# Mixing spread over five steps, sums moved to GpSimd, two products exchanged

## The chip, the cores and the metric

One core of a Trainium2 chip runs the whole program. The metric is the device time of one execution in microseconds; several executions were timed, and one was profiled. The engines go by their short names: PE is TensorE (PEld its weight loads), DVE is VectorE, ACT is ScalarE, POOL is GpSimd, and SP issues most DMAs.

## The reference, cut to what matters

```python
# attention, 8 batches x 8 heads, 576 rows of 64
scores = scale * q @ k.T
scores = where(scores >= max(scores) - tau, scores, -1e9)
x = concat_heads(softmax(scores) @ v)              # (8, 576, 512)
# mixing and channel block
mixed = real(fft(fft(x, axis=1), axis=2))
u = x + mixed
un = (u - mean(u)) / sqrt(var(u) + 1e-6)           # over the 512 channels
out = u + relu(un @ w_ch1) @ w_ch2                 # 512 -> 2048 -> 512
```

## The kernel before, in words

**Attention.** The loop over i runs through 160 steps: 8 batches of 4 head pairs (`NPAIR`) of 5 row tiles (`NT`). In step i, `scores(i)` multiplies one tile of q with the pair's k into two PSUM tiles (`sc`, L434 and L445), and `softmax(i)` takes the row maxima on DVE (`neg`, L462), the exponentials on ACT (`e`, L470), the threshold with the row sum on DVE (L478), and the division (L494). The weights of step i - 1 are transposed on PE (`pe`, `pw`, L540 and L559) and copied out by ACT (`ends`, `e_t`, L547 and L561). When the weights of two tiles stand, `weighted_values(n, 0)` multiplies the first 256 rows with v (`pv`, L582) in the pair's third step (t = 2); `weighted_values(n, 1)` does the other 320 in the first step of the next pair (t = 0). The result goes from PSUM into `x`, a tile of its own for each of the four pairs of a batch (`x0` to `x3`, one buffer each, L588 or L590).

**Folding.** `fold_rows` adds and subtracts a pair's x with its mirror image in a room called `half` (L615; one buffer, also used for `swap`, through which two rows change places by four DMAs in pairs of odd number) and writes `f` (L620 to L629). It runs on POOL, for the last pair of a batch on DVE.

**Mixing.** `mixing(b)` is a generator. It first combines f on DVE (L644 to L672), and yields three times for that. Then come eleven units, a yield behind each: six `py` products over the channels (L683, copied by ACT into `y_e` and `y_o`, L688 and L693) and five `pa`/`pb` products over the sequence (L700, L704). The second sort is followed by ACT's copy into `tmp` (L715; one buffer), two DVE operations (L719, L720) and POOL's additions of x into `u_t` (L722, L726). `u_t` is u transposed, a ring of two batches. Mixing reads all four x tiles of its batch until its last additions are done.

**Channel work.** Groups of 256 rows (16 of them, from g = 2 on) compute both products with seven instead of eight block products; the other blocks' sums make up for the eighth. In `hidden_in_quarters`, `sums` forms the sums of u's quarters (`t_u`, and one block of `u_t` in place, L891), `weights` the sums of the first weights (`s_w`, L900), and `product(m, part)` one of seven products (`ph`, L917) for one half of the hidden units. Products 1, 6 and 7 accumulate in one PSUM bank that is held from 1 to 7; DVE adds what they give to `hs` (L926), ACT copies or applies the relu (L931 and on). Groups alternate between two orders: up starts with product 5, down with product 3. The output stage `channels_in_quarters` does the same for the second product (`po`, L1058), with POOL's `s_form` (L1054), DVE's `combine` (L1019) and DVE's `rows.add` (L795). All matmuls but the scores share four PSUM banks (tag `mm`).

**Order.** From step 40 on, PE executes in the order in which the program is written; a planner orders the other engines' queues, taking what is ready in its own reckoning by order of writing. Up to step 40 all engines keep the written order. Between the parts of a step stand three calls of `fill()`, called stretches here. Each adds `per_slot` to a budget, takes units of mixing and then units of channel work until the budget is spent; channel work of batch b is allowed once its mixing is finished (`mixed`). `start_batch(b)` appends a batch's mixing and groups at the end of the step with i % 20 == 0. Then:

```python
if i < total:
    mix(3)
    pace = iter((0, 2, 2, 2, 2, 4))
```

that is, DVE's part at once, nothing in the next stretch, and then two units in each of four stretches and the rest in the sixth. The last batch (i = 160) has no pace and takes one unit per stretch.

Of the kernel before, what the change touches and what calls it, by code (L numbers as in the profile page):

```python
# [9 lines left out]
FP32 = mybir.dt.float32  # L10
INT32 = mybir.dt.int32
UINT32 = mybir.dt.uint32
ALU = mybir.AluOpType
# [34 lines left out]
def kernel(  # L48
# [12 lines left out]
    nc = tc.nc  # L61
    B, H, S, D = q.shape
# [3 lines left out]
    NPAIR = H // 2  # L66
# [316 lines left out]
    xs = {}  # L383
# [184 lines left out]
    def weighted_values(n, part):  # L568

        b, p = n // NPAIR, PAIRS[n % NPAIR]  # L570
        _, _, vt, e_t, ends, recs = heads[n]
        if part == 0:
            if n % NPAIR == 0:
                xs[b] = [None] * NPAIR
            xs[b][p] = sb.tile([128, S], FP32, tag=f"x{p}", bufs=1, name=f"x{p}")
        x = xs[b][p]
        m = (256, S - 256)[part]
        cols = slice(256 * part, 256 * part + m)
        pv = ps.tile([128, 512], FP32, tag="mm", bufs=4, name="pv")
        for c in range(5):  # L580
            for j in range(2):
                nc.tensor.matmul(  # L582
                    pv[64 * j : 64 * j + 64, 0:m], vt[:, 2 * c + j, :],
                    e_t[:, 4 * j + c, 0:m] if c < 4 else ends[:, 0:m],
                    start=(c == 0), stop=(c == 4), skip_group_check=True,
                )
        if normalized(n):
            nc.scalar.copy(x[:, cols], pv[:, 0:m])  # L588
        else:
            nc.vector.tensor_tensor(  # L590
                out=x[:, cols], in0=pv[:, 0:m], in1=recs[:, 0:m], op=ALU.mult
            )
        if part == 0:
            return
        heads.pop(n)
        if p % 2:

            swap = sb.tile([2, S], FP32, tag="half", bufs=1, name="swap")
            for j in range(2):
                nc.sync.dma_start(out=swap[j : j + 1, :], in_=x[64 * j : 64 * j + 1, :])  # L600
            for j in range(2):
                nc.sync.dma_start(out=x[64 * j : 64 * j + 1, :], in_=swap[1 - j : 2 - j, :])
# [276 lines left out]
    def hidden_in_quarters(g, rows, quarter):  # L879


        c0 = tokens_of(g)[0] % RING
        c1 = (c0 + 128) % RING
        up = (g - FIRST) % 2 == 0
        b = [[[u_t[:, 2 * k + c, z : z + 128] for c in range(2)] for z in (c0, c1)]
             for k in range(2)]
        t1, t2, minus_t4 = ([t_u[:, m, c, :] for c in range(2)] for m in range(3))

        def sums(out_, in0, in1):
            for c in range(2):  # L890
                nc.vector.tensor_tensor(out=out_[c], in0=in0[c], in1=in1[c], op=ALU.subtract)  # L891

        sums(t1, b[0][1], b[0][0])
        sums(t2, b[1][1], t1)
        sums(minus_t4, b[1][0], t2)

        def weights(eng, part, in0, in1, op=ALU.subtract):
            cols = slice(512 * part, 512 * part + 512)
            for c in range(2):
                eng.tensor_tensor(  # L900
                    out=s_u[c][:, cols], in0=in0[c][:, cols], in1=in1[c][:, cols], op=op
                )

        OPERANDS = {
            1: (a_w1[0][0], b[0][0]), 2: (a_w1[0][1], b[1][0]), 3: (s_u, b[1][1]),
            4: (a_w1[1][1], minus_t4), 5: (s_u, t1), 6: (s_u, t2), 7: (a_w1[1][0], b[0][1]),
        }
        banks = {}

        def product(m, part):  # L910
            name = "sum" if m in (1, 6, 7) else m
            if m not in (6, 7):
                banks[name] = ps.tile([128, 512], FP32, tag="mm", bufs=4, name="ph")
            left, right = OPERANDS[m]
            for q in range(4):
                for c in range(2):
                    nc.tensor.matmul(  # L917
                        banks[name][:, 128 * q : 128 * q + 128],
                        left[c][:, 512 * part + 128 * q : 512 * part + 128 * q + 128], right[c],
                        start=q == 0 and c == 0 and m not in (6, 7), stop=c == 1,  # L920
                        skip_group_check=True,
                    )
            return banks[name][:, :]

        def add(to, bank, other=None):
            nc.vector.tensor_tensor(  # L926
                out=to, in0=bank, in1=to if other is None else other, op=ALU.add
            )

        def relu(to):  # L930
            nc.scalar.activation(out=to, in_=to, func=ACT.Relu)  # L931

        def fifth(part):
            y = product(5, part)
            h01, h11 = quarter(1, 0, part), quarter(1, 1, part)
            if up:
                nc.scalar.copy(h11, y)

                weights(nc.gpsimd, part, s_u, a_w1[0][0])
            else:  # L940
                add(h01, y)
                relu(h01)
                add(h11, y)
                relu(h11)

        def third(part):
            y = product(3, part)
            h01 = quarter(1, 0, part)
            if up:
                add(h01, y)  # L950
                relu(h01)
            else:
                nc.scalar.copy(h01, y)
                weights(nc.gpsimd, part, a_w1[1][1], a_w1[1][0])

        def first_two(part):
            h00 = quarter(0, 0, part)
            nc.scalar.copy(h00, product(1, part))
            yield 4096
            add(h00, product(2, part))  # L960
            relu(h00)
            yield 4096

        def others(part):
            h10, h01, h11 = quarter(0, 1, part), quarter(1, 0, part), quarter(1, 1, part)
            x = product(6, part)
            add(h01, x, h11 if up else None)

            if up:
                weights(nc.vector, part, a_w1[0][1], s_u)  # L970
            else:
                weights(nc.vector, part, s_u, a_w1[0][0], ALU.add)
            yield 4096
            nc.scalar.copy(h10, product(4, part))
            yield 4096
            x = product(7, part)
            add(h10, x)
            relu(h10)
            if up:
                add(h11, x)  # L980
                relu(h11)
            else:
                nc.scalar.copy(h11, x)
            yield 4096

        begin, end = (fifth, third) if up else (third, fifth)
        begin(0)
        yield 4096
        yield from first_two(0)
        rows.load(1)  # L990

        sums(b[0][1], b[1][1], b[0][1])
        yield ND * 128
        yield from others(0)
        begin(1)
        yield 4096
        rows.load(0)
        yield ND * 128
        yield from first_two(1)
        end(0)  # L1000
        yield 4096
        rows.factors(0, 2)
        yield from others(1)
        end(1)
        yield 4096
# [117 lines left out]
    mixes = []  # L1123
    mixed = 0
    work = []
    pace = iter(())
    spent = budget = per_slot = 0.0
    per_batch = NPAIR * NT

    def fill():  # L1130
        nonlocal budget, spent
        budget += per_slot
        if mixes:
            mix(next(pace, 1))
        while work and spent < budget and work[0][0] < mixed:
            done = next(work[0][1], None)
            if done is None:
                work.pop(0)
            else:
                spent += done  # L1140

    total = B * per_batch
# [203 lines left out]
    for i in range(2 * per_batch, total + 1):  # L1346
        if i < total:
            scores(i)
            softmax(i)

        n, t = divmod(i, NT)
        nothing = iter(())
        prep = prep_in_parts(n + 1) if t == 3 and n + 1 < B * NPAIR else nothing
        weights = weights_in_parts(i - 1)
        next(prep, None)
        fill()
        next(weights, None)
        fill()
        next(weights, None)
        next(prep, None)  # L1360
        fill()
        next(prep, None)
        if t == 2:
            weighted_values(n, 0)
        if t == 0:
            weighted_values(n - 1, 1)
            for _ in fold_rows(n - 1):
                pass
            if n + 1 < B * NPAIR:
                load_v(n + 1)  # L1370
        if i % per_batch == 0:
            start_batch(i // per_batch - 1)
            if i < total:

                mix(3)
                pace = iter((0, 2, 2, 2, 2, 4))
    per_slot = cost(0) / 40
    while mixes or work:
        fill()
# [46 lines left out]
```

## Time and profile before

| | |
|---|---|
| time, median of 3 runs | 1706.87 us (1705.91 to 1709.2) |
| profiled run | 1705.85 us, span of its trace 1704.1 us |
| PE busy | 1631.2 us, 96% |
| DVE busy | 1224.0 us, 72% |
| ACT busy | 775.4 us, 46% |
| POOL busy | 616.4 us, 36% |
| DMA | 57.5 MB, 34 GB/s on average |

A line of a group or of the timeline names an engine, the line of the kernel, the operation, what is written and read, and its size; in brackets stands the idle time of the engine just ahead of it and what ended it. "PE pw L559 <- DVE qT L400" reads: PE sat idle before the transposes into `pw` until DVE had written `qT`. In a table of windows, "(x90)" is the number of instructions, and the column behind POOL is the clock that PE was granted, 1.00 being full.

### The profile page before, as it was taken

What the parts mean: (1) busy time and instruction counts of PE and PEld (TensorE: products, weight loads), DVE (VectorE), ACT (ScalarE), POOL (GpSimd) and SP (SyncE); (2) the same over time, 40 slices, a digit from 0 to 9 for tenths busy, and PEclk for the clock granted to TensorE, in tenths of its full rate; (3) what the DMA queues carried; (4) which work ended last, traced back from release to release, by engine and by line L of the source; (5) the groups of instructions that cost most, each with busy time, mean ns of one, the idle gap of its engine ahead of it and who ended that gap; (6) DMA issues with size and microseconds to landing.
All of it is one profiled execution on the core that took longest, in us unless ns stands there. A gap on an engine that the chain in (4) does not pass through costs nothing.

```text
span 1704.1 us, 29009 instructions
## 1 busy us (share of the span) xinstructions
PE 1631.2 (96%) x10838; PEld 1283.4 (75%) x10838; DVE 1224.0 (72%) x2822; ACT 775.4 (46%) x1735; POOL 616.4 (36%) x707
## 2 busy tenths in 40 slices
PE   8998899899999999999999899999999999989998
PEld 4555555567787787878788778777878788878998
DVE  6885885657767887767677777778687778654555
ACT  5764675433545363625354535353545445422111
POOL 5673463212324333233442334333241425232333
PEclk9999999999999999999999999999999999999999
DMA  5323222010010101101011010100111010000000
GB/s 161 111 54 108 71 72 55 14 34 21 19 38 18 28 12 41 22 15 33 15 29 28 19 33 9 38 22 22 28 29 34 16 34 2 13 1 13 13 13 13
DMA packets 130386, 57.50 MB, mean 34 GB/s; under 512 B 121123, under 2 KB 121125, under 8 KB 130246
## 3 DMA queue, kind: packets, MB, share of 16 engines
q1 hardware_dynamic: 128854, 55.35, 12.0%
q8 instruction: 86, 1.41, 0.3%
q14 instruction: 54, 0.44, 0.1%
q10 hardware_dynamic: 1392, 0.30, 0.1%
HBM read 46.02 MB, written 9.44 MB: 33 GB/s over the span
## 4 chain that ended last, share of the span: by engine, by line
PE 76%; DVE 12%; ACT 7%; POOL 3%; issue 2%; DVEq 0%; ACTq 0%; POOLq 0%
PE po L1058 22%; PE ph L917 21%; PE pv L582 8%; PE sc L434 7%; PE pw L559 6%; PE po L839 3%; DVE e L478 2%; DVE neg L462 2%; ACT e L470 2%; PE sc L445 2%; POOL u_t L722 1%; PE ph L813 1%; PE py L683 1%; POOL u_t L726 1%; PE pd L112 1%
## 5 line engine op out<-in xcount | busy, mean ns | idle before, releaser
L470 ACT ACTIVATE e<-sc,neg 128x576 f32<-128x576 f32 x288 | 211.7, 735 | 264.5 <-DVE neg L462 264.0
L462 DVE TENSOR_REDUCE neg<-sc 128x1 f32<-128x576 f32 x288 | 206.4, 751 | 139.6 <-PE sc L434 126.8
L478 DVE SCALAR_TENSOR_TENSOR e<-sc,thr,e 128x576 f32<-128x576 f32 x288 | 227.2, 814 | 57.8 <-ACT thr L474 55.3
L1058 PE MATMUL po<-w,hs 128*128 128x256 f32 x1024 | 244.6, 385 | 2.3 <-DVE u L795 2.2
L1058 PEld LDWEIGHTS po<-w,hs 128*128 128x128 f32 x1024 | 187.9, 191 | 35.3 <-issue 9.4
L917 PE MATMUL ph<-u_t,w 128*128 128x128 f32 x1536 | 189.7, 279 | 6.7 <-DVE hs L926 4.8
L917 PEld LDWEIGHTS ph<-u_t,w 128*128 128x128 f32 x1536 | 180.5, 194 | 10.3 <-DVE hs L926 5.1
L559 PE MATMUL pw<-ident,e 128*128 128x128 f32 x1152 | 170.7, 275 | 17.2 <-DVE qT L400 7.0
L561 ACT COPY e_t<-pw 128x512 f32<-128x512 f32 x256 | 148.4, 593 | 79.6 <-PE pw L559 79.2
L434 PE MATMUL sc<-kT,qT 64*128 64x288 f32 x1024 | 166.9, 429 | 6.7 <-DVE e L478 6.0
L926 DVE TENSOR_TENSOR hs<-ph,hs 128x512 f32<-128x512 f32 x160 | 107.3, 685 | 77.0 <-PE ph L917 51.3
L559 PEld LDWEIGHTS pw<-ident,e 128*128 128x128 f32 x1152 | 134.7, 141 | 35.4 <-DVE qT L400 7.7
L434 PEld LDWEIGHTS sc<-kT,qT 64*128 64x128 f32 x1024 | 92.0, 186 | 67.3 <-issue 41.0
L1054 POOL TENSOR_TENSOR s_tile<-hs 128x512 f32<-128x512 f32 x32 | 52.8, 1649 | 243.9 <-ACT hs L931 243.9
L494 DVE TENSOR_SCALAR e<-e,den 128x576 f32<-128x576 f32 x216 | 135.2, 663 | 2.6
L917 PE MATMUL ph<-t_u,s_w 128*128 128x128 f32 x1024 | 125.2, 276 | 0.0
L795 DVE SCALAR_TENSOR_TENSOR u<-po,rstd,u 128x256 f32<-128x256 f32 (+1 forms) x164 | 75.8, 484 | 66.0 <-PE po L1058 62.9
L917 PEld LDWEIGHTS ph<-t_u,s_w 128*128 128x128 f32 x1024 | 119.1, 192 | 4.4 <-issue 2.3
L900 POOL TENSOR_TENSOR s_w<-s_w,w 128x512 f32<-128x512 f32 x32 | 40.9, 1300 | 223.1 <-PE ph L917 211.6
L1058 PE MATMUL po<-hs,s_tile 128*128 128x256 f32 x512 | 121.1, 382 | 0.0
L931 ACT ACTIVATE hs<-hs 128x512 f32<-128x512 f32 x128 | 80.0, 632 | 86.8 <-DVE hs L926 86.4
L900 POOL TENSOR_TENSOR s_w<-w,w 128x512 f32<-128x512 f32 x32 | 40.0, 1272 | 211.5 <-PE ph L917 211.5
(192 smaller groups left out, 2950.8 us busy)
## 6 DMA issues: line engine op xcount, KB each, us to landing
hs<-in_moe_w_ch_dram SPq DMA_DIRECT2D x23, 512.0 KB, 4.3
out_dram<-u SPq DMA_DIRECT2D x36, 256.0 KB, 2.1
qk_in<-in_q_dram SPq DMA_DIRECT2D x64, 128.0 KB, 2.2
v_in<-in_v_dram SPq DMA_DIRECT2D x64, 128.0 KB, 2.4
qk_in<-in_k_dram SPq DMA_DIRECT2D x31, 128.0 KB, 2.5
w<-in_moe_w_ch_dram SPq DMA_DIRECT2D x6, 512.0 KB, 8.0
qk_in<-in_k_dram SPq DMA_DIRECT2D x31, 64.0 KB, 2.2
stage<-in_moe_w_ch_dram SPq DMA_DIRECT2D x3, 512.0 KB, 3.8
```

The source lines that it names most:

```text
L434: nc.tensor.matmul(sc[j][:, c, 0:HALF], qT[hp, 128 * t : 128 * t + 128], kT[hp, HALF * c : HALF * (c + 1)], start=True, stop=True,)
L462: nc.vector.tensor_reduce(out=neg[:, j : j + 1], in_=sc[j][:, :, 0:HALF], axis=AXIS_XY, op=ALU.max, negate=True,)
L470: nc.scalar.activation(out=ej, in_=sc[j][:, :, 0:HALF], func=ACT.Exp, bias=neg[:, j : j + 1], scale=1.0)
L478: nc.vector.scalar_tensor_tensor(out=ej, in0=sc[j][:, :, 0:HALF], scalar=thr[:, j : j + 1], in1=ej, op0=ALU.is_ge, op1=ALU.mult, accum_out ...
L494: nc.vector.tensor_scalar(out=e[:, S * j : S * (j + 1)], in0=e[:, S * j : S * (j + 1)], scalar1=den[:, j : j + 1], scalar2=None, op0=ALU.mult,
L559: nc.tensor.transpose(pw[:, c, :], e[:, c0 : c0 + 128], ident[:, :])
L561: nc.scalar.copy(e_t[:, 4 * j : 4 * j + 4, qs], pw[:, :, :])
L582: nc.tensor.matmul(pv[64 * j : 64 * j + 64, 0:m], vt[:, 2 * c + j, :], e_t[:, 4 * j + c, 0:m] if c < 4 else ends[:, 0:m], start=(c == 0), ...
L900: eng.tensor_tensor(out=s_u[c][:, cols], in0=in0[c][:, cols], in1=in1[c][:, cols], op=op)
L917: nc.tensor.matmul(banks[name][:, 128 * q : 128 * q + 128], left[c][:, 512 * part + 128 * q : 512 * part + 128 * q + 128], right[c], start ...
L926: nc.vector.tensor_tensor(out=to, in0=bank, in1=to if other is None else other, op=ALU.add)
L1058: nc.tensor.matmul(bank[:, 0 : DM // 2], left[p], right[p], start=start and p == 0, stop=p == NK - 1, skip_group_check=True,)
```

## The change

It has four parts.

- Mixing takes one unit in every stretch, so that it starts in the first stretch of step i + 1 and ends in the last of step i + 5. `mix(3)` and `pace` go.
- Because the first pair's x would be written (part 0, step i + 2) while mixing still reads the old x of the same tile, part 0 of a batch's first pair goes into a tile of the tag `half`. With part 1 the tile `x` proper is taken, and POOL copies the 256 columns over. This holds for all eight batches.
- `sums` runs on POOL instead of DVE. In turn, `weights` for part 0 of the up groups runs on DVE instead of POOL.
- In the up groups, part 0 begins with product 1, then 5, then 2 (5, 1, 2 before). The other orders stay: part 1 and the down groups are only written differently.

```diff
 def weighted_values(n, part):
-        if part == 0:
+        m = (256, S - 256)[part]
+        if n % NPAIR == 0 and part == 0:
+            xs[b] = [None] * NPAIR
+            x = xs[b][p] = sb.tile([128, m], FP32, tag="half", bufs=1, name="x_first")
+        else:
+            x = xs[b][p]
+            if x is None or n % NPAIR == 0:
+                x = sb.tile([128, S], FP32, tag=f"x{p}", bufs=1, name=f"x{p}")
             if n % NPAIR == 0:
-                xs[b] = [None] * NPAIR
-            xs[b][p] = sb.tile([128, S], FP32, tag=f"x{p}", bufs=1, name=f"x{p}")
-        x = xs[b][p]
-        m = (256, S - 256)[part]
+                nc.gpsimd.tensor_copy(x[:, 0:256], xs[b][p][:, :])
+            xs[b][p] = x
...
         def sums(out_, in0, in1):
             for c in range(2):
-                nc.vector.tensor_tensor(out=out_[c], in0=in0[c], in1=in1[c], op=ALU.subtract)
+                nc.gpsimd.tensor_tensor(out=out_[c], in0=in0[c], in1=in1[c], op=ALU.subtract)
...
-                weights(nc.gpsimd, part, s_u, a_w1[0][0])
+                weights(nc.gpsimd if part else nc.vector, part, s_u, a_w1[0][0])
...
-        begin(0)
+        for one in (first, begin) if up else (begin, first):
+            one(0)
+            yield 4096
+        second(0)
         yield 4096
-        yield from first_two(0)
         rows.load(1)
...
-        yield from first_two(1)
-        end(0)
-        yield 4096
+        for one, part in ((first, 1), (second, 1), (end, 0)):
+            one(part)
+            yield 4096
...
-    pace = iter(())
...
         if mixes:
-            mix(next(pace, 1))
+            mix(1)
...
             start_batch(i // per_batch - 1)
-            if i < total:
-
-                mix(3)
-                pace = iter((0, 2, 2, 2, 2, 4))
```

`first` and `second` are the two halves of the former `first_two`.

More of the change, by code (lines that the diff above doesn't have):

```diff
@@ L954, in third, with first, second @@
                 weights(nc.gpsimd, part, a_w1[1][1], a_w1[1][0])
-        def first_two(part):
+        def first(part):
+            nc.scalar.copy(quarter(0, 0, part), product(1, part))
+        def second(part):
             h00 = quarter(0, 0, part)
-            nc.scalar.copy(h00, product(1, part))
-            yield 4096
             add(h00, product(2, part))
             relu(h00)
-            yield 4096
         def others(part):
@@ L998, in hidden_in_quarters @@
         yield ND * 128
-        yield from first_two(1)
-        end(0)
-        yield 4096
+        for one, part in ((first, 1), (second, 1), (end, 0)):
+            one(part)
+            yield 4096
         rows.factors(0, 2)
```

## The prediction

> **What bounds the kernel now.** I read the page's busy shares first, then the windows view, then the waits of TensorE, then the timeline around the longest of them.
>
> ```profile
> PE 1631.2 (96%) x10838; PEld 1283.4 (75%) x10838; DVE 1224.0 (72%) x2822; ACT 775.4 (46%) x1735; POOL 616.4 (36%) x707
> ```
>
> TensorE is busy 1631 of 1704 us and no other engine comes near, so a change that leaves TensorE's work alone (this one does: no matmul is added or removed) can win at most its idle time and the time it runs at a lower clock. The windows view says where the idle time lies. These six windows are the steps i+1 to i+3 behind each batch's last attention step i = 40, 60, 80, 100, 120 and 140 (step starts are read off the timeline at the score matmuls L434), where the mixing runs. Columns: window, length, busy us of PE, PEld, DVE, ACT and POOL, granted clock.
>
> ```profile
> 304.50:342.70 38.20, 32.51 (x186) 20.49 (x184) 26.46 (x64) 17.40 (x39) 8.60 (x12) 1.00 0.05 15
> 518.10:549.10 31.00, 28.53 (x234) 24.03 (x232) 24.38 (x61) 17.86 (x39) 13.35 (x15) 1.00 0.05 11
> 701.80:744.00 42.20, 38.33 (x266) 32.25 (x264) 32.92 (x76) 19.29 (x41) 17.61 (x18) 0.92 0.04 8
> 940.20:974.20 34.00, 28.87 (x234) 24.04 (x232) 27.58 (x66) 17.24 (x38) 12.21 (x14) 1.00 0.04 9
> 1125.50:1161.10 35.60, 30.48 (x233) 25.65 (x231) 27.66 (x66) 17.25 (x38) 12.27 (x14) 0.95 0.04 9
> 1312.40:1346.40 34.00, 28.87 (x234) 24.04 (x232) 27.57 (x66) 17.25 (x38) 12.29 (x14) 1.00 0.04 10
> sum 215.00, PE 187.59 PEld 150.49 DVE 166.57 ACT 106.29 POOL 76.32; mean PE 31.26 PEld 25.08 DVE 27.76 ACT 17.72 POOL 12.72
> ```
>
> Idle: 215.0 - 187.6 = 27.4 us. Clock: 8% of 42.2 and 5% of 35.6, 5.2 us. The mixing stretches cost 32.6 us. Between them there is next to nothing: 1178.5 to 1301.5 us has 122.76 busy of 123.0, with the same attention and channel work. Who ends the waits, in the stretch from 1125.5 to 1161.1:
>
> ```profile
> PE pw L559 <- DVE qT L400: 2.3, 1, 2.3
> PE pv L582 <- ACT tmp L715: 1.4, 1, 1.4
> PE py L683 <- ACT ends L547: 0.7, 1, 0.7
> ```
>
> The timeline shows what VectorE did ahead of that qT:
>
> ```profile
> 1150.04 0.87 DVE L891 TENSOR_TENSOR t_u<-u_t,t_u 128x128 f32<-128x128 f32 x1 [1.87 <-POOL u_t L722]
> ...
> 1151.49 0.77 DVE L891 TENSOR_TENSOR t_u<-u_t,t_u 128x128 f32<-128x128 f32 x1 [0.58 <-POOL u_t L722]
> 1152.18 1.41 DVE L462 TENSOR_REDUCE neg<-sc 128x1 f32<-128x576 f32 x2
> 1153.52 0.74 DVE L400 TENSOR_SCALAR qT<-pq,q_scale 128x512 f32<-128x512 f32 x1
> 1154.31 0.66 PE L559 MATMUL pw<-ident,e 128*128 128x128 f32 x4 [2.33 <-DVE qT L400]
> ```
>
> The sums of u's quarters (L891), which no product reads before 1210.7 us, stand in VectorE's queue and wait for GpSimd's additions into u_t; the row maxima and qT wait behind them, and TensorE behind those. The 1.4 us is another chain: L715 waits 3.6 us for GpSimd to let go of tmp. Last, the end of the kernel, where mixing already runs one unit per stretch with work in between (timeline, then windows):
>
> ```profile
> 1505.08 3.78 PE L917 MATMUL ph<-u_t,w 128*128 128x128 f32 x16 [4.33 <-DVE hs L926]
> 1539.91 5.41 PE L1058 MATMUL po<-w,hs 128*128 128x256 f32 x16 [2.17 <-DVE u L795]
> ```
>
> ```profile
> 1505.00:1512.20 7.20, 7.12 (x40) 7.12 (x41) 1.92 (x5) 1.60 (x4) 0.00 (x0) 0.62 0.00 0
> 1539.90:1545.50 5.60, 5.59 (x18) 4.62 (x19) 0.82 (x3) 0.00 (x0) 0.00 (x0) 0.70 0.12 47
> ```
>
> Neither wait there is for a py or pa step: interleaved mixing does not stall on itself. The second is again VectorE late with L891 ahead of it. Both are followed by a low clock: (1 - 0.62) x 7.2 = 2.7 and (1 - 0.70) x 5.6 = 1.7 us.
>
> **What the skill says.** GPSIMD Engine Reference, section 8 (Key points): GpSimd shares its SBUF interfaces with VectorE and contends with VectorE instructions that have two SBUF inputs. The trace agrees: L891 takes 267 ns at least and up to 1357, the long ones beside GpSimd's L722 and L1054. So sums on GpSimd do not come free to VectorE, but they no longer block its queue. TensorE: Matmul & The Clock Gate, Part 1, has the clock at half after an idle window of about 3.4 us; here 2.2 to 4.3 us of waiting were enough (the rows above), and after an equal 2.3 us at step 143 the clock stayed at 1.00. I count it as likely for gaps over 2 us.
>
> **The change, part by part.**
>
> *Mixing in one unit per stretch.* Before: the fold's VectorE work at the end of step i, then 11 units of matmuls in steps i+1 and i+2 with little or no channel work between. After: VectorE's part in the first stretch of step i+1, two stretches with no mixing, then one unit in each of 11 stretches, to the second of step i+5. Channel work of this batch starts only when mixing has ended, so older work must last. Counted in the code's own units: 15 stretches x 4154 = 62,300, less 19,240 of mixing, is 43,100, and 0.4 x 198,144 = 79,300 is kept (for batch 3, whose stretch is 6082: 72,000). It lasts. From step i+6 the order is as before. What stays, from step 121's rows: the product into the held bank (product 7, after product 6) now comes in step i+1, ahead of py, and waits until VectorE has read product 6. That addition (L926) ran at 1134.9 to 1135.5, after the fold, the seven f steps (4.0 us) and softmax, whose order hardly changes. TensorE would be there at about 1134.0: product 6 ends at 1130.4, transposes 0.7, bank wait 0.7, product 4 1.8, transposes 0.5. Gap about 1.5 us, in the five batches from the second on (the first has no quarters yet): 7.5 us. Bounds: 0, if softmax runs earlier, to the 4.33 + 2.7 = 7.0 of the tail each. The bank wait (py <- ends L547, 0.7) passes to product 4: 6 x 0.7 = 4.2 us. Kept together: 11.7.
> New: from step i+3 on the four banks hold an output product, the held sum and a mixing unit, leaving one for transposes. The trace of before shows such waits at 0.2 to 0.3 us (L683 behind y_o and f), about three a batch: 0.7 x 6 = 4.2 us; bounds 0 and three times that. Mixing issues no DMA; on GpSimd its additions move in among the L1054 forms, with a unit's distance between them and L715.
>
> *First part of x in the folds' room.* It takes away the wait of x (ACT L588 for POOL u_t L726: 10.8 us, 6 times) that would otherwise hold ScalarE for three steps. It adds a copy on GpSimd per batch, 128x256, between L500 (128x128, 390 ns) and L535 (128x630, 808 ns): 0.5 us x 8 = 4 us. Queued behind it: the swap's two pairs of DMAs on SP, which wait for the room, and the fold, needed five steps later at the earliest. On TensorE's path nothing; the ScalarE copy of x's second part still waits for GpSimd's additions, which have about 6 us: counted at nothing, bounds 0 to 1.4 x 6 (the old L715 wait). In the first two batches, where all queues keep the written order, it adds the copy and takes one such wait away: nothing, bounds -1.7 (a gap behind L715 at 160.7 us) to +1.
>
> *Sums by GpSimd.* 128 instructions leave VectorE: 25.9 + 21.8 + 8.8 = 56.5 us. On GpSimd each is near L620's 486 ns (128x143): 63 us. All hidden: GpSimd is free 64% of the time and the sums are issued up to 60 us ahead. What it gives is counted in the stretches above, and the tail's 2.17 + 1.7 = 3.9 us.
>
> *p1 in front of p5; half the weight sums to VectorE.* 16 of L900 leave GpSimd (16 x 1.3 = 21 us) for VectorE (16 x 0.69 = 11 us). p1 needs no sum, so a late t1 has a product's time (1.8 us) and a stretch. p6 now follows p5 by one product instead of two: VectorE has 2 x 0.69 us to do in at least 2.5 us. Nothing; bounds 0 to 8 x 1.5.
>
> Sum: -32.6 - 3.9 + 11.7 + 4.2 = -20.6 us. From the profiled span, 1704.1 to 1683.5; its own run took 1705.85, the three timed ones 1705.91 to 1709.2. From their median, 1706.87 - 20.6 = 1686.
>
> **The rivals.** *Clean (0.17):* the stretches become like their neighbours; all 36.5 us go: 1670. For it: neighbours with equal load idle 0.2 us; against: the fold and f steps still crowd VectorE in step i+1. *Moved (0.09):* product 7 and banks take back nearly all: 1703 to 1709. *Slower (0.13):* product 7 behind VectorE's fold in every one of the five batches as in the tail, 7.0 us each with the clock, 35, plus banks 4.2 and, at the upper bound of the bank term, 12.6: 36.5 - 51.8, or +15, 1722; at the middle bank term +7, 1714. It decides from (36.5 - 8.4) / 5 = 5.6 us of wait per batch. For it, the same three instructions in the same order at 1505; against, there no attention work (about 3 us of TensorE time) lies between product 6 and 7. *Not what it says:* channel work runs out during mixing; excluded by the count above.
>
> **How the numbers follow.** The forecast has 0.61, its own range 1678 to 1694 from the bounds of the two kept terms. 1669 to 1707 leaves out the slower case and a little below. 0.2% is 3.4 us, about what a measurement of this kernel can tell. Faster: 0.61 + 0.17; same 0.09; slower 0.13.
>
> **What would show it.** VectorE near 1179 us, GpSimd near 663 (616 + 63 - 21 + 4); no L891 on VectorE; steps i+2 to i+5 with under 1 us idle; a gap of 1 to 2 us ahead of product 7 (ph<-u_t,w behind hs L926) in step i+1; the tail's 4.33 still there, its 2.17 gone. It would be wrong if the gap at product 7 passed 5 us, or if TensorE waited for L891 or L1054.

## The result, and the profile after

| | median us | runs |
|---|---|---|
| before | 1706.51 | 1705.91 to 1709.2 (4) |
| after | 1722.42 | 1721.79 to 1723.7 (4) |

The ratio is 1.0091, with a 95% interval from 1.0074 to 1.0109: the change makes the kernel 16 us slower. The forecast was 20 us faster. The profiled execution after has a span of 1721.0 us, 16.9 above the one before.

The page's busy shares, first line:

```profile
PE 1639.9 (95%) x10838; PEld 1288.7 (75%) x10838; DVE 1187.5 (69%) x2710; ACT 776.9 (45%) x1735; POOL 655.1 (38%) x827
```

VectorE lost 36.5 us and GpSimd gained 38.7, with 112 instructions fewer and 120 more: the work moved as the change says. TensorE has the same 10838 instructions and is busy 8.7 us longer; a lower clock accounts for 5.4 of that. (In the kernel after, lines from the mixing on have moved by six: the additions L926 are L932, the products L917 L923, f's L663 to L672 are L669 to L678, the sums L891 are L897. GpSimd's forms L1054 have moved by eight, to L1062.)

Mixing now lasts five steps. The windows view of the kernel after, over steps i+1 to i+5 of the six batches (length, busy PE, PEld, DVE, ACT, POOL, granted clock):

```profile
306.70:365.05 58.35, 53.46 (x264) 30.22 (x263) 32.00 (x82) 22.35 (x51) 11.65 (x19) 0.97 0.09 25
521.81:576.19 54.38, 48.47 (x333) 39.18 (x331) 39.48 (x92) 24.00 (x53) 22.00 (x26) 0.97 0.08 17
710.99:773.98 62.99, 59.07 (x388) 47.52 (x386) 43.78 (x104) 24.74 (x53) 26.32 (x29) 1.00 0.07 15
947.76:1003.12 55.36, 48.07 (x333) 39.02 (x331) 41.19 (x91) 22.96 (x51) 20.04 (x25) 0.97 0.07 17
1137.05:1193.27 56.22, 48.80 (x332) 39.56 (x330) 41.49 (x91) 22.87 (x51) 20.04 (x25) 0.94 0.07 17
1327.20:1383.77 56.57, 49.43 (x333) 39.73 (x331) 41.22 (x91) 22.96 (x51) 20.05 (x25) 0.94 0.07 17
sum 343.87, PE 307.29 PEld 235.23 DVE 239.16 ACT 139.88 POOL 120.09; mean PE 51.22 PEld 39.20 DVE 39.86 ACT 23.31 POOL 20.01
```

The same six stretches took 327.35 us before, with PE busy for 299.94. So 16.5 of the 16.9 us lie here: idle time rose from 27.4 to 36.6 us, and what the clock costs (its shortfall, times the time in which TensorE was busy) from 4.8 to 10.1 us. Elsewhere the tail won 3.1 and the first two batches lost 2.2, within the scatter of 2 us that starts show.

TensorE's waits in the kernel after, over the whole run (in total, times, longest):

```profile
PE ph L923 <- DVE hs L932: 25.7, 9, 5.1
...
PE ph L923 <- ACT y_e L699: 4.2, 4, 1.1
...
PE py L689 <- ACT y_e L699: 2.5, 1, 2.5
...
PE ph L923 <- ACT ends L547: 2.4, 2, 1.2
```

The first line was 6.1 us before. All but 1.8 us of it is product 7, which goes into the held bank behind product 6, waiting for VectorE's addition of product 6. The three qT waits of 7.0 us, which led the list before, are gone; one of 0.8 us is left. Step 121, timeline of the kernel after:

```profile
1140.11 1.95 PE L923 MATMUL ph<-t_u,s_w 128*128 128x128 f32 x16
...
1142.00 0.60 PE L559 MATMUL pw<-ident,e 128*128 128x128 f32 x4
...
1142.44 1.95 PE L923 MATMUL ph<-t_u,w 128*128 128x128 f32 x16
...
1144.01 1.27 POOL L1062 TENSOR_TENSOR s_tile<-hs 128x512 f32<-128x512 f32 x1 [12.26 <-ACT hs L937]
1144.23 0.60 PE L559 MATMUL pw<-ident,e 128*128 128x128 f32 x4
...
1144.36 1.26 DVE L669 TENSOR_TENSOR f<-sums 128x304 f32<-128x304 f32 x1
...
1145.36 1.37 POOL L1062 TENSOR_TENSOR hs<-hs 128x512 f32<-128x512 f32 x1
...
1145.60 1.47 DVE L675 SCALAR_TENSOR_TENSOR f<-sums,factors 128x304 f32<-128x304 f32 x1
...
1147.50 0.94 DVE L494 TENSOR_SCALAR e<-e,den 128x576 f32<-128x576 f32 x2
...
1149.19 0.68 DVE L932 TENSOR_TENSOR hs<-ph,hs 128x512 f32<-128x512 f32 x1
1149.92 3.78 PE L923 MATMUL ph<-u_t,w 128*128 128x128 f32 x16 [5.09 <-DVE hs L932]
```

The product at 1140.11 is product 6, that at 1142.44 is product 4. TensorE is through with product 4 and the transposes at 1144.8 and has nothing but product 7 to do. VectorE works all this time, on f (L669 to L678) and on softmax; the addition that product 7 waits for stands behind them. Product 7 then takes 3.78 us instead of 1.95: the clock has dropped to half (0.50 from 1149.9 to 1153.7). Gaps of this kind in steps 61, 81, 101, 121 and 141 are 2.40, 2.40, 4.88, 5.09 and 4.83 us, 19.6 together. The tail's is unchanged, and its 2.17 us ahead of `po` is gone:

```profile
1525.02 3.78 PE L923 MATMUL ph<-u_t,w 128*128 128x128 f32 x16 [4.34 <-DVE hs L932]
```

### The profile page after: what moved, and what is told of

Same layout as the page of the kernel before. It is cut to its first block, busy times and chain, and to the rows that moved or that the text cites. A ratio compares the mean times of both kernels' runs of the same rounds, so it can differ in the third digit from the quotient of the medians.

```text
span 1721.0 us, 28994 instructions
## 1 busy us (share of the span) xinstructions
PE 1639.9 (95%) x10838; PEld 1288.7 (75%) x10838; DVE 1187.5 (69%) x2710; ACT 776.9 (45%) x1735; POOL 655.1 (38%) x827
## 4 chain that ended last, share of the span: by engine, by line
PE 77%; DVE 12%; ACT 7%; issue 2%; POOL 1%; DMA 1%; SPq 0%; DVEq 0%; ACTq 0%; POOLq 0%
PE po L1066 22%; PE ph L923 21%; PE pv L588 8%; PE sc L434 7%; PE pw L559 5%; PE po L845 3%; DVE e L478 2%; ACT e L470 2%; DVE neg L462 2%; PE sc L445 2%; PE ph L819 1%; PE py L689 1%; PE pa L706 1%; PE pd L112 1%; PE pa L710 1%
## 5 line engine op out<-in xcount | busy, mean ns | idle before, releaser
L478 DVE SCALAR_TENSOR_TENSOR e<-sc,thr,e 128x576 f32<-128x576 f32 x288 | 226.9, 813 | 52.5 <-ACT thr L474 52.0
L923 PE MATMUL ph<-u_t,w 128*128 128x128 f32 x1536 | 196.6, 284 | 28.1 <-DVE hs L932 24.4
L923 PEld LDWEIGHTS ph<-u_t,w 128*128 128x128 f32 x1536 | 186.1, 199 | 34.2 <-DVE hs L932 25.9
L932 DVE TENSOR_TENSOR hs<-ph,hs 128x512 f32<-128x512 f32 x160 | 107.2, 684 | 78.0 <-PE ph L923 60.0
L801 DVE SCALAR_TENSOR_TENSOR u<-po,rstd,u 128x256 f32<-128x256 f32 (+1 forms) x164 | 75.8, 482 | 85.4 <-PE po L1066 82.5
L494 DVE TENSOR_SCALAR e<-e,den 128x576 f32<-128x576 f32 x216 | 129.3, 635 | 2.8
L923 PE MATMUL ph<-t_u,s_w 128*128 128x128 f32 x1024 | 125.2, 276 | 1.1 <-ACT y_e L699 1.0
L1062 POOL TENSOR_TENSOR s_tile<-hs 128x512 f32<-128x512 f32 x32 | 45.6, 1425 | 209.3 <-ACT hs L937 154.7
L923 PEld LDWEIGHTS ph<-t_u,s_w 128*128 128x128 f32 x1024 | 119.0, 192 | 5.1 <-issue 1.9
L1066 PEld LDWEIGHTS po<-hs,s_tile 128*128 128x128 f32 x512 | 93.7, 190 | 13.7 <-issue 2.6
```

Source lines behind the costliest of these rows:

```text
L478: nc.vector.scalar_tensor_tensor(out=ej, in0=sc[j][:, :, 0:HALF], scalar=thr[:, j : j + 1], in1=ej, op0=ALU.is_ge, op1=ALU.mult, accum_out ...
L494: nc.vector.tensor_scalar(out=e[:, S * j : S * (j + 1)], in0=e[:, S * j : S * (j + 1)], scalar1=den[:, j : j + 1], scalar2=None, op0=ALU.mult,
L923: nc.tensor.matmul(banks[name][:, 128 * q : 128 * q + 128], left[c][:, 512 * part + 128 * q : 512 * part + 128 * q + 128], right[c], start ...
L932: nc.vector.tensor_tensor(out=to, in0=bank, in1=to if other is None else other, op=ALU.add)
L1066: nc.tensor.matmul(bank[:, 0 : DM // 2], left[p], right[p], start=start and p == 0, stop=p == NK - 1, skip_group_check=True,)
```

## The experiments

Theory: spreading the mixing took the py products out from between product 6 and product 7, so that product 7 waits for VectorE, with f's steps ahead of the addition. The other parts are good or neutral. Rivals: the sums on GpSimd cost VectorE more than they give; bank waits of the spread units and the clock do the harm.

**Half of the change each.** The sums, the weights and the order of p1 alone, with mixing as before:

```diff
-                nc.vector.tensor_tensor(out=out_[c], in0=in0[c], in1=in1[c], op=ALU.subtract)
+                nc.gpsimd.tensor_tensor(out=out_[c], in0=in0[c], in1=in1[c], op=ALU.subtract)
...
-                weights(nc.gpsimd, part, s_u, a_w1[0][0])
+                weights(nc.gpsimd if part else nc.vector, part, s_u, a_w1[0][0])
...
+        for one in (first, begin) if up else (begin, first):
```

> The kernel before with only the last two parts of the change: sums of u's quarters on GpSimd, part 0's weight sums of the up groups on VectorE, product 1 ahead of 5. Mixing keeps its pace and x its room. Theory Q (the loss is product 7 waiting for VectorE's addition of product 6, which the spread mixing brings together with the fold and the f steps; the sums on GpSimd help): no wait over 1 us ahead of product 7 in step i+1; the waits of 2.3 to 2.9 us for qT in steps 83, 103, 123 and 143 and the tail's 2.17 us go, with their low clock; faster than before by 10 to 19 us, 1688 to 1697. Rival P (the sums or the weight sums on their new engines delay products in all groups): slower than before by 8 us or more, with PE waits for L891, L900 or L1054 spread over the groups.

And mixing with x's room alone, that is, the kernel after with these three edits undone:

> The kernel before with only the first two parts: mixing in one unit per stretch, and x's first part in the folds' room. Sums stay on VectorE, the weight sums on GpSimd, product 5 ahead of 1. Theory Q: product 7 waits as after the change, 2.4 to 5 us in five batches with the low clock behind it; slower than before by 10 to 25 us, 1717 to 1732. Rival P: no loss, 1680 to 1700.

Measured: 1692.02 us, ratio 0.9922 (0.9908 to 0.9935), and 1730.95 us, ratio 1.0141 (1.0124 to 1.0159). The sums' half wins 13.8 us, the mixing's half loses 25.1. Their sum, +11.3, is 4.6 us short of the change's +15.9. In the mixing's half the waits of product 7 are 2.40 to 4.83 us, with VectorE's sums where they were: the sums are not their cause.

**The sums alone**, before with only the first two lines of that diff:

> The kernel before with one edit: sums of u's quarters on GpSimd. Weight sums and the products' order as before. Theory Q: VectorE's queue no longer waits for GpSimd's additions to u_t, which is all that e1 gained: 1692 within 2.5. Rival: the exchange of products 1 and 5 and the weight sums carry part of it, then 1695 to 1704; or they cost, then under 1689.

Measured: 1690.44 us, ratio 0.9901 (0.9886 to 0.9916). All of the half's gain is the sums'; the weights and the order add nothing. The medians differ by 1.6 us the wrong way, and the two intervals overlap. In the traces, step 52 is 0.7 us longer with these two edits and steps 69 and 99 are 0.4 us longer each, which is a small cost; the first 40 steps, which the edits do not touch, differ by 2.0 us.

**f one stretch later** in the kernel after; py and pa stay where they were.

```diff
     def mixing(b):
...
+        yield 0
         E, O = slice(0, FW), slice(FW, 2 * FW)
         fold_chunks(nc.vector, b, 0)
...
-        for _ in range(3):
+        for _ in range(2):
             yield 0
```

> The changed kernel with mixing's VectorE part (f) taken one stretch later, behind products 3 and 6 instead of ahead of them; the number of stretches stays, two empty ones become one behind it. Theory Q: VectorE adds product 6 ahead of most of f, the wait of product 7 falls from 2.4 to 5.1 us to under 1.5 us in the five batches and the clock stays up; faster than after by 15 to 30 us, 1692 to 1707. Rival P, or a loss spread over the units of mixing (banks): within 4 us of after, 1718 to 1726.

Measured: 1693.95 us, ratio 0.9927 (0.9915 to 0.994), 28.5 us under the kernel after with no other edit. The timeline of its step 121 (it begins at 1126.40) shows the order that the edit makes:

```profile
1131.79 1.95 PE L924 MATMUL ph<-t_u,w 128*128 128x128 f32 x16
...
1133.71 0.68 DVE L933 TENSOR_TENSOR hs<-ph,hs 128x512 f32<-128x512 f32 x1
...
1134.45 2.05 PE L924 MATMUL ph<-u_t,w 128*128 128x128 f32 x16 [0.27 <-DVE den L483]
...
1137.65 0.46 DVE L670 TENSOR_TENSOR f<-sums 128x304 f32<-128x304 f32 x1
```

The addition comes before f's steps, product 7 waits 0.27 us instead of 5.09 and takes 2.05 instead of 3.78. Over the six mixing windows the length falls by 21.9 us, from 343.87 to 322.01, and the tail's by 5.3. The price is a new, smaller wait, of py behind f (6.5 us in all) and behind VectorE's additions (3.3).

**The dose.** Two more VectorE operations in mixing (the maximum of a value with itself, so nothing changes but the time) lie ahead of product 6's addition:

```diff
+        if b >= 2:
+            for _ in range(2):
+                nc.vector.tensor_tensor(out=s01[:, 0, :], in0=s01[:, 0, :], in1=s01[:, 0, :], op=ALU.max)
```

> The changed kernel with two VectorE instructions more in the f steps (the maximum of a sum with itself, 128x608, written to its place: the output stays the reference's), from the third batch on, ahead of VectorE's addition of product 6. Each is near 0.7 to 0.8 us by the row of L650. Theory Q (TensorE waits at product 7 for that addition, and the clock falls with it): each of the six waits, the tail's among them, grows by 1.4 to 1.6 us: 1722 + 9 = 1731, up to 1735 where GpSimd holds them up. Rival (the wait is set by something else, or VectorE has room ahead of the addition): 1722 within 3.

Measured: 1731.65 us, ratio 1.0142 (1.0128 to 1.0156). Against their own runs of the kernel before, the kernel after loses 15.9 us and this one 24.4: 8.5 us more. The timeline of its step 121 and of its tail:

```profile
1156.57 3.57 PE L926 MATMUL ph<-u_t,w 128*128 128x128 f32 x16 [6.50 <-DVE hs L935]
...
1533.02 3.78 PE L926 MATMUL ph<-u_t,w 128*128 128x128 f32 x16 [5.80 <-DVE hs L935]
```

All six gaps (those of the five steps and the tail) grew by 1.4 to 1.5 us, 8.5 together. VectorE's time ahead of that addition goes into the time of the kernel one for one; nothing absorbs it.

**The tail by itself**: the sums' half with the same edit of the generator as above. In the batches that have the pace this leaves everything in place, since `mix(3)` takes all three yields at once; only the last batch changes.

> The kernel of e1 (old pace, sums on GpSimd) with f taken one stretch later in the mixing generator. With the old pace's three units at once this changes nothing in the seven attention batches; only the last batch's mixing, at the tail, takes f behind products 3 and 6. Theory Q: the tail's wait of 4.33 us ahead of product 7 with its low clock goes, as it did in e3 (tail 222.2 to 217.9 us); 1692.0 - 4.5 = 1687, against e1's 1692. Rival: the tail's gain in e3 came from the spread mixing's other order; then 1692 within 1.5.

Measured: 1685.31 us, ratio 0.987 (0.9857 to 0.9884). The tail's 4.34 us wait is gone (0.4 is left), py waits 1.4 for f, and the tail runs 4.6 us shorter than in the sums' half (222.2 to 217.6). The whole run gains 6.7, of which 1.8 lie in the first 40 steps, where both kernels do the same.

**A later f with later units**: in the kernel after, f and all that follows one stretch later, except in the first batch.

```diff
+        if b > 0:
+            yield 0
         E, O = slice(0, FW), slice(FW, 2 * FW)
```

> The changed kernel with f one stretch later, as e3, and one more empty stretch between f and the first unit of matmuls, so that mixing ends one stretch later. Theory Q: in e3 the first units still wait for f (0.45 to 3.04 us, py behind DVE f) and for y_e; these go and the clock stays up: e3's 1694 less 5 to 10, 1684 to 1689. Rival B (banks: spread mixing costs PSUM banks wherever it stands): the waits move to the next transposes and units, 1691 to 1697.

Measured: 1706.15 us, ratio 0.999 (0.9982 to 0.9998), far off the 1684 to 1689 that were expected. Product 7's waits are down to 2.3 us in all and the tail is the shortest of all (215.9 us), yet it is 12.2 us behind the run with f alone moved. Mixing ends a stretch later, and GpSimd's sums now meet VectorE's combinations in step i+6 (timeline at step 126; the four combinations with their least, median and longest time in ns; then TensorE's waits):

```profile
1187.67 1.69 POOL L899 TENSOR_TENSOR t_u<-u_t,t_u 128x128 f32<-128x128 f32 x4
...
1188.34 3.66 DVE L1029 TENSOR_TENSOR hs<-hs,w 128x256 f32<-128x256 f32 x2
...
1189.34 1.26 POOL L1064 TENSOR_TENSOR hs<-hs,s_tile 128x512 f32<-128x512 f32 x1
...
1190.69 0.70 POOL L535 COPY v_rev<-v_in 128x630 f32<-128x630 f32 x1
```

```profile
L1029 DVE TENSOR_TENSOR hs<-hs,w x4: 407/410/3328, 1188.3 to 1193.9; 128x256 f32<-128x256 f32 x4
```

```profile
PE pw L559 <- ACT ends L547: 7.1, 6, 1.7
...
PE pw L559 <- ACT tmp L723: 5.3, 5, 1.7
```

Of the four combinations, the first takes 3.33 us and the others 0.41 each. The first ends at 1191.67, just behind GpSimd's last instruction of an unbroken run (1191.39); the row threshold L478 stands behind it until 1191.93. Steps 66, 67, 107, 127 and 147 together are 11.7 us longer than with f alone moved, 3.4 of them by a low clock in step 67. That this hold-up of VectorE is the whole cause of the pw waits was not tried.

**Does spreading give anything?** The kernel after with the generator's edit and f, as in the kernel before, at the end of step i; then py two at a time and pa one at a time:

```diff
+    pace = iter(())
...
-            mix(1)
+            mix(next(pace, 1))
...
             start_batch(i // per_batch - 1)
+            if i < total:
+                mix(3)
+                pace = iter((0, 2, 2, 2))
```

> The changed kernel with the old start of mixing (f at the end of step i, then two units in each of three stretches, the six py) and one unit per stretch from there on for the five pa; tail as e4. Theory Q: no product 7 behind f, since py comes first and uses the channel work's budget, and the wait of 1.0 to 2.0 us for tmp (pv behind L715) goes, as the pa come one stretch apart: e4 less 3 to 9, 1678 to 1684. Rival B (banks): a unit of mixing among the output products costs 1.3 us a batch, as in step 125 of after: 1684 to 1690.

And the same with `pace = iter((0,))`, so that py is spread too:

> The kernel of e7 with f at the end of step i as before the change, an empty stretch, and one unit in every stretch from then on, the py too. Theory Q (the spread itself costs nothing; the place of f ahead of products 6 and 7 does): products 6 and 7 come after some py, product 6's addition after f all the same, so that product 7 waits little, under 1.5 us: 1677 to 1686, near e7. Rival B (one unit of mixing per stretch costs banks and waits by itself): 1690 or more.

Measured: 1678.82 us, ratio 0.983 (0.9817 to 0.9844), and 1693.43 us, ratio 0.9913 (0.9899 to 0.9926). The first is as hoped: its mixing windows are 305.4 us long and idle 10.6, the least so far, at a full clock. Against the run that tried the tail by itself, which has the sums and the later f in the tail but the old pace (1685.31 us), it wins 6.5 us: that is what spreading pa gives, together with x's room. The second is not as hoped: py one at a time costs 14.6 us. Of that 6.6 lie in steps 41 to 45 (4.3 of these by a low clock), about 1.1 in each of the other five batches' windows, and 1.2 in each of steps 107, 127 and 147. Product 7 is innocent here (2.1 us in all); TensorE's waits of the second:

```profile
PE pe L540 <- DVE e L494: 4.6, 3, 1.5
PE pw L559 <- ACT ends L547: 4.1, 5, 1.0
PE py L690 <- ACT y_e L700: 4.1, 5, 2.9
```

So there is no single wait behind it; each spread unit shifts what follows, and small waits come up in new places.

**The best of these without the weights' edit**: py two at a time as above, with part 0's weight sums on GpSimd and product 5 first again.

```diff
-                weights(nc.gpsimd if part else nc.vector, part, s_u, a_w1[0][0])
+                weights(nc.gpsimd, part, s_u, a_w1[0][0])
...
-        for one in (first, begin) if up else (begin, first):
+        for one in (begin, first):
```

> The kernel of e7 with the fourth part of the change undone: product 5 ahead of 1 again, all weight sums of the up groups on GpSimd. e6 and e1 differed by 1.6 us in favour of leaving that part out: 1677 within 2 (e7: 1678.8). If that difference was chance: 1678.8 within 2 as well, and the part is worth nothing; if the exchange is needed once mixing is spread: over 1681.

Measured: 1674.39 us, ratio 0.9808 (0.9795 to 0.9822). This is 33 us faster than the kernel before and 48 faster than the kernel after. Of the 4.4 us to the run above with py two at a time, 3.1 lie in the first 40 steps, which this part does not touch; a low clock cost TensorE 6.6 us there in that run and 1.7 in this one. Steps 52, 69 and 99 are again shorter by 0.7, 0.4 and 0.4 us. So undoing this part is worth about 1.5 us, seen in two pairs of traces and too little for the timed runs to show. Most of the 4.4 us is the scatter of the start.

## Why the prediction was wrong

**The step that failed** is "Gap about 1.5 us, in the five batches from the second on", priced at 7.5 us, and in it "whose order hardly changes". Both sides of the estimate were read off the kernel before. TensorE's arrival was put 8.5 us after the step's start and was 7.8 in step 121. The addition was to end 10.0 us after the start, as before, and ended 12.8 after it. Two items make up nearly all of these 2.8 us. The normalisation L494 (0.94) now comes before the addition. In the kernel before it stood behind it:

```profile
1134.86 0.69 DVE L926 TENSOR_TENSOR hs<-ph,hs 128x512 f32<-128x512 f32 x1
...
1136.12 0.95 DVE L494 TENSOR_SCALAR e<-e,den 128x576 f32<-128x576 f32 x2
```

And f's steps, written one part later than before, met GpSimd's s_form: L669 and the first L675 took 1.26 and 1.47 us, where in step 61 of the kernel after, with no GpSimd work beside them, they took 0.47 and 0.53, together 1.7 us less:

```profile
529.03 0.47 DVE L669 TENSOR_TENSOR f<-sums 128x304 f32<-128x304 f32 x1
...
529.48 0.53 DVE L675 SCALAR_TENSOR_TENSOR f<-sums,factors 128x304 f32<-128x304 f32 x1
```

TensorE's arrival 0.7 earlier and the addition 2.8 later turn the forecast's 1.5 us into the 5.1 of step 121. Moving f alone (28.5 us back) and lengthening VectorE's queue alone (8.5 us more) show the mechanism from both sides; the split of the 2.8 us is read, not tried.

**The sum, term by term**, for the mixing windows and the tail:

| term | forecast us | measured us |
|---|---|---|
| old stretches' idle and clock | -32.6 | -32.2 |
| product 7, idle | +7.5 | +19.6 |
| banks, old and new, and other idle | +8.4 | +17.0 |
| clock in the new stretches | 0 | +10.1 |
| busy time that the clock does not explain | 0 | +2.0 |
| tail | -3.9 | -3.1 |
| sum | -20.6 | +13.4 |

(17.0 is 36.6 - 19.6.) Product 7 is the larger part of the error: 12.1 us of idle time and 8.4 of the clock, 20.5 of 34.0 us. (The other 1.7 of the clock follows the wait of py in step 42.) The forecast counted a gap of 1.5 us, with no clock lost behind it; gaps of 2.4 to 5.1 us brought a low clock in four steps of five. The Trainium skill (TensorE: Matmul & The Clock Gate, Part 1) speaks of half the clock after an idle window of about 3.4 us. The trace agrees for the three gaps near 5 us. Of the two gaps of 2.40 us, one was followed by a product of 3.61 us and the other by one of 2.05; the last section shows what tells them apart.

The bank term was too small by a factor of two: product 5 or 1 behind `y_e` in steps i+2 (4.2 us), products behind `ends` in steps 61 and 81 (2.4), `py` behind `y_e` in step 42 (2.5), and two small waits in steps i+5 (5.2). It came out at its upper bound, 12.6 and the 4.2 of the old waits. That these are all waits for banks is read from the code (these products do not read the tiles whose copying they wait for), not tried.

**The rival that came nearest** is "Slower": product 7 behind VectorE in all five batches, deciding from 5.6 us of wait and clock per batch. Measured, with the clock of these five batches, it is (19.6 + 8.4) / 5 = 5.6. So product 7, with the banks as forecast, took back all that the change was to win; the waits beyond the forecast's bank term, the clock after step 42 and the busy time made the loss. The argument against this rival, about 3 us of attention work on TensorE between products 6 and 7, had a wrong reading in it: product 4 (1.95 us) was counted in, which stands between them in the tail too (at 1498.79 before). The attention's own work there is the transposes at 1141.9 and 1144.2, about 1.2 us. And in VectorE's queue the same attention puts L478 to L494, about 2.5 us, ahead of the addition. The wrong inference is older: in the kernel before, product 7 came in step i+3 because the py units filled the stretches. Taking them out moved product 7 to where VectorE is busiest, and the forecast priced this wait from the old queue's times.

**What held.** The sums on GpSimd alone gave 17 us, in the way that was forecast: none is left on VectorE, and the 7.0 us of qT waits and the tail's `po` wait are gone. One sign of being wrong showed here all the same, though small: TensorE waited for a sum on GpSimd once (1.6 us, at 432.1) and for a form once (0.3). On GpSimd the 128 sums take 31.6 + 15.0 + 14.4 = 61.0 us (63 was the estimate). VectorE is at 1187.5 us (1179), GpSimd at 655.1 (663). x's first part in the folds' room showed no wait of TensorE; GpSimd's folds waited longer for the swaps behind it (82.5 us in all, 33.8 before), at no visible cost. Two other signs failed: the gap at product 7 was to stay within 5 us and passed it in step 121, and steps i+2 to i+5 were to be idle for under 1 us, where five of the six batches have 2.3 to 4.5. The tail kept its 4.34.

## What to carry to other kernels

Before work is spread out, ask what stood between two instructions that depend on each other through a slow engine: the block that is moved away may have been the cover of another wait. Read the arrival at such a wait from the new order of both queues, with contention and the clock's drop, not from the old times. When a change bundles several edits, price them apart: here the best kernel keeps the sums, x's room and a half-spread mixing, and is 48 us faster than the bundle.

## What was not expected of the hardware

**VectorE and GpSimd held each other up whole, not by a factor.** In the kernel after, seven operations of f started while a form of GpSimd ran, the 1.26 and 1.47 us of step 121 among them. All seven ended 0.33 us after the form that they had met. The combination of 3.33 us ended 0.28 us after GpSimd's run. It went the other way too: GpSimd's form at 465.42 took 3.28 us, against a median of 1.29, while VectorE did six combinations at its usual pace.

```profile
L1062 POOL TENSOR_TENSOR s_tile<-s_tile,hs x48: 1254/1290/3277, 465.4 to 1706.1; 128x512 f32<-128x512 f32 x48
465.47 2.10 DVE L1027 TENSOR_TENSOR hs<-w,w 128x256 f32<-128x256 f32 x6
```

The Trainium skill (GPSIMD Engine Reference, section 8, Key points) states that GpSimd contends with VectorE instructions that have two SBUF inputs. What it cost in these cases was the rest of the other engine's work, and ahead of a wait of TensorE that is lost in full.

**The clock's drop followed a fixed grid.** The traces record the granted clock. Between 300 us and the end of the work it is either full or half, and half comes in stretches of 3.41 us or twice that. In the kernel after they begin at 325.12, 533.34, 960.00, 1147.74, 1338.88 and 1523.20 us, whole multiples of 3.413 us apart. Divide the twelve traces into windows on their grids, and each of the 35 windows at full clock in which TensorE was idle for 1.99 us or more is followed by one at half. With less idle time only two were (1.35 us with early f and py one at a time, 1.80 in the mixing's half). So a gap costs clock or not by how it falls. Step 61's 2.40 us lie nearly all in one window, step 81's are split (length and busy PE; the clock is the third column from the end):

```profile
529.92:533.34 3.42, 1.14 (x11) 0.90 (x9) 3.42 (x10) 1.58 (x3) 0.00 (x0) 1.00 0.00 0
533.34:536.75 3.41, 3.29 (x15) 3.30 (x16) 1.26 (x3) 0.12 (x1) 3.06 (x2) 0.50 0.00 0
...
717.66:721.07 3.41, 2.49 (x20) 2.25 (x20) 3.41 (x12) 1.59 (x4) 0.00 (x0) 1.00 0.00 0
721.07:724.49 3.42, 1.85 (x16) 1.85 (x17) 2.71 (x5) 0.63 (x1) 1.76 (x1) 1.00 0.00 0
724.49:727.90 3.41, 3.41 (x29) 2.81 (x28) 2.08 (x4) 1.77 (x4) 2.92 (x3) 1.00 0.00 0
```

This also settles the forecast's open case, two waits of 2.3 us of which one kept the clock: it was split into 0.9 and 1.4 us (step 143 before), the other was not (2.2 us from 1152.10 on).
